# Re-timing the first group of a fused DeltaNet and maxout kernel: conversions, key-query products and substitution steps

## The chip, the cores and the metric

The kernel runs on one core of a Trainium2 chip. The metric is the device time of one execution in microseconds (us), the median of several runs. A profile is one more execution, recorded by the hardware profiler; its own time is given beside its span (from the first to the last instruction).

## The reference

Two blocks follow each other. The first is a delta-rule recurrence over 4 batches x 8 heads, 768 tokens of 48 dimensions; the second a maxout layer with three weight matrices of 384 x 768 and an output matrix of 768 x 384, applied to the 3072 tokens. Everything is float32.

```python
# attention: q, k, v are (4, 8, 768, 48), beta is (4, 8, 768)
k_n = k / (np.linalg.norm(k, axis=-1, keepdims=True) + 1e-06)
for t in range(S):
    kt, vt, bt = (k_n[:, :, t], v[:, :, t], beta[:, :, t, None])
    y[:, :, t] = np.einsum('bhd,bhde->bhe', q[:, :, t], state)
    v_old = np.einsum('bhde,bhd->bhe', state, kt)
    state = state + bt[:, :, :, None] * np.einsum('bhd,bhe->bhde', kt, vt - v_old)
# bridge: (B,H,S,D) -> (B*S, H*D), then
h = np.maximum(np.maximum(x @ w1, x @ w2), x @ w3)
return h @ w_out
```

## The kernel before

**Tiling.** The 768 tokens are cut into 12 chunks of 64, two chunks to a group; the six groups (m = 0 to 5) are pipelined. Within a chunk the recurrence becomes matrix products, so that the work on one chunk is a chain of small products. A unit is one chunk of half the batches: group m has units 4m to 4m+3. With its 4 batches a group gives 256 tokens a chunk, and the maxout layer works on 512 tokens (`TOK`) at a time: group m's maxout is interleaved with the recurrence of group m+1 and the substitution of group m+2.

**The recurrence, unit by unit and chunk by chunk.** `turn(n)` transposes the keys (part 0) or the queries (part 1) of unit n on TensorE; ScalarE copies the result. `gram(n)` (L427) multiplies keys by keys (part 0, the scores "at") and keys by queries (part 1, the masked "pt": the key-query product; the mask is a VectorE instruction, L422). The tiles at, pt, the transposed "t" and the maxout's hidden "h" share one pool of 17 buffers called "square" (L339): a new one waits until an old one's last reader is done. Then, for chunk c, come `halves_z`, `halves_u`, `join_z`, `turn_t1` and `join_u` (e, f, z, d, j: joining the inverted blocks), `old_k` and `old_q` (k, q: the state's part), `new` (u), `step` (s: the state's update), `to_y` (y) and `to_x` (x: the transposed output, input of the maxout layer). The tables `LINKS`, `EARLY_LINKS` and `FIRST` name them by such a letter and a chunk of the group (z0, z1), t and g with a unit (t0 to t3, g0 to g3).

**The substitution.** `solve(m)` (L521) inverts 32 x 32 triangular blocks of group m on VectorE: norms first, then 31 steps of two instructions (L565 multiplies into tmp, L569 subtracts from y), each bracketed by a resumption of the generator; then y goes to DRAM (L591, two DMAs) and comes back re-laid as ut (L600, eight DMAs). For m = 1 its input x and its result y lie in the SBUF space of the output weights `wo_sb`, which are written there only later: `in_wo(0)` is its first 1056 elements of a row, `in_wo(1)` the next 1056. For the other groups they are tiles of their own, `x_bl` and `y_bl`, with one buffer each. Group 0 has a shorter version, done before the stretch in question.

**The weights.** The weights come in 24 pieces of 128 x 384: for each f (128 of the 768 hidden columns) one of each of the three matrices, then six pieces of the output matrix. `fetch` (L211) issues the DMA of a piece on SyncE into one of five buffers; `weights` (L221) converts one: three ScalarE instructions (L238 to L240), and for the piece before it one VectorE shift (L250) and one integer addition on GpSimd (L254, the join). `less_first(f)` (L880) subtracts the first matrix's columns from those of the other two on VectorE (L883); the maxout uses the differences, and adds the first matrix back through `turn_first` and `both_layers`, its product with the output matrix.

**The maxout of group 0.** `ffn(m)` (L915) is a generator. A piece is one `hidden` product for one f and one difference: three products, evicted by ScalarE (L934) for the first difference and by VectorE (L938) for the second. Their PSUM tiles have two buffers, so a piece waits for the eviction of the one two before it. In group 0 four f's are done in narrow pieces of 256 tokens, first the eight for chunk 0's tokens, then the eight for chunk 1's, which need x1; f = 4 and 5 are four wide pieces of 512 tokens. Three `both_layers` products and eight half blocks of output (L959) follow. After each, control returns to the loop at L1152, whose body number i issues what the tables hold for i.

**What sets the order.** All of this stands in an order written out by hand (L95 to L1201): each engine runs its instructions in the order in which the program emits them, and each DMA queue issues in its order. The loop body emits, in this order: fetches, steps that go ahead, `FIRST`, `EARLY_LINKS`, conversions, the other steps, differences, turns of the first matrix, value scaling, and loads.

Of the kernel before, what the change touches and what calls it, by code (L numbers as in the profile page):

```python
# [23 lines left out]
def kernel(  # L24
# [177 lines left out]
                (w_t[:, :, cols], bits[:, :, f * 256 : (f + 1) * 256], (KT, 128))  # L202
            )
    bits = moe_w_out.bitcast(U32).rearrange("(t p) f -> p t f", p=128)
    for t in range(FT):
        pieces.append((wo_sb[:, t : t + 1], bits[:, t : t + 1], (1, DM)))

    staged = deque()
# [272 lines left out]
    def in_wo(i):  # L481
        n = BL * BL + BL
        return wo_sb.rearrange("p t d -> p (t d)")[:, n * i : n * (i + 1)].rearrange(
            "p (s r) -> p s r", s=2
        )
# [32 lines left out]
        )  # L518


    def solve(m):  # L521


        x = in_rows(xs[m])
        if m == 1:
            y_bl = in_wo(1)
        else:
            y_bl = work.tile([128, 2, HB * BL + HB], FP32, name="y_bl", bufs=1)
            if m > 2:
                zero = kpad[0][:, 0:1, D : D + 1]  # L530
                nc.scalar.copy(y_bl, zero.to_broadcast(y_bl.shape))
            else:
                nc.gpsimd.memset(y_bl, 0.0)
        y = in_rows(y_bl)
        bl = small("bl", BL)
        norm(bl, diagonal(x), small("root_bl", BL), small("nt_bl", BL))
        if m:
            norms_of(m, bl)
        nc.vector.reciprocal(bl, bl)
        nc.vector.tensor_tensor(out=bl, in0=bl, in1=bl, op=ALU.mult)  # L540
        nc.vector.tensor_tensor(out=bl, in0=bl, in1=beta_bl[:, m] if m else beta_0, op=ALU.mult)
        (nc.scalar.copy if m > 2 else nc.gpsimd.tensor_copy)(diagonal(y), bl)
        if m < FINE:
            size, xv, yv = HB, in_blocks(xs[m]), in_blocks(y_bl)
            xb = xv[:, :, :, 0:HB]
            by = bl.rearrange("p (s i) -> p s i", i=HB)[:, :, None, :]
            by = by.to_broadcast([128, 2, HB, HB])
        else:
            size, xv, yv = BL, x[:, None], y[:, None]
            xb, by = x, bl[:, None, :].to_broadcast([128, BL, BL])  # L550
        nc.vector.tensor_tensor(out=xb, in0=xb, in1=by, op=ALU.mult)
        yield
        for j in range(size - 1):
            a, b = j + 1, size - 1 - j
            n = BL // size
            tmp = work.tile([128, 256], FP32, name="tmp")
            t_v = tmp[:, 0 : n * a * b].rearrange("p (s c i) -> p s c i", s=n, i=b)
            row, column, rest = (
                xv[:, :, j, None, j + 1 : size],
                yv[:, :, 0:a, j, None],  # L560
                yv[:, :, 0:a, j + 1 : size],
            )
            if n == 1:
                row, column, rest, t_v = (t[:, 0] for t in (row, column, rest, t_v))
            nc.vector.tensor_tensor(  # L565
                out=t_v, in0=row.to_broadcast(t_v.shape),
                in1=column.to_broadcast(t_v.shape), op=ALU.mult,
            )
            nc.vector.tensor_tensor(out=rest, in0=rest, in1=t_v, op=ALU.subtract)  # L569
            yield  # L570
        if m == 0:
            back = in_rows(xs[0])
            nc.vector.transpose(out=back, in_=y.rearrange("p c i -> p i c"))
            yield
            for cc in range(2):
                for i in range(4):
                    bb, half = divmod(i, 2)
                    r = block(bb, half)
                    to = ut[cc][r, :, :, BL * half : BL * (half + 1)].rearrange(
                        "p g h i -> p (g h) i"  # L580
                    )
                    of = back[r, :, 16 * cc : 16 * (cc + 1)].rearrange("p i x -> p x i")
                    if half:
                        nc.scalar.copy(to, of)
                    else:
                        (nc.gpsimd if cc else nc.vector).tensor_copy(to, of)
                yield
            return
        y_d = dram.tile([2, 2, B, H, BL, BL], FP32, name="y_d")
        for cc in range(2):  # L590
            nc.sync.dma_start(  # L591
                out=y_d[cc].rearrange("f b h i j -> (f b h) i j"),
                in_=y[64 * cc : 64 * (cc + 1)],
            )
        yield
        for cc in range(2):
            for half in range(2):
                for bb in range(2):
                    r0 = C * bb + BL * half
                    (one_queue if m or cc else both_queues)[bb].dma_start(  # L600
                        out=ut[cc][
                            r0 : r0 + BL, :, :, BL * half : BL * (half + 1)
                        ].rearrange("p g h i -> p (g h) i"),
                        in_=y_d[cc, half, 2 * bb : 2 * bb + 2].rearrange(
                            "b h c i -> c (b h) i"
                        ),
                    )
            yield
# [32 lines left out]
    def halves_t(c):  # L641

        fine[c] = [square("t") for g in range(2)]
        src = [ut[c % NU][:, g].rearrange("p h x -> p (h x)") for g in range(2)]
        dst = [t.rearrange("p h x -> p (h x)") for t in fine[c]]
        nc.vector.transpose(out=dst[0], in_=src[0])
        for bb in range(2):
            nc.vector.transpose(out=dst[1][rows(1 - bb)], in_=src[1][rows(bb)])
# [266 lines left out]
    def ffn(m):  # L915
# [24 lines left out]


        early = 4 if m == 0 else 0
        for lo in (0, TOK // 2):
            for f in range(early):
                yield from hidden(f, lo, TOK // 2)
        for f in range(early, FT):
            yield from hidden(f, 0, TOK)
        if m == 0:
# [24 lines left out]
    def some(gen, n):  # L973
        for _ in range(n):
            if next(gen, gen) is gen:
                break
# [53 lines left out]
    turn(6, (0,))  # L1030
    turn(0, (1,))
    load_q(3, (nc.gpsimd, nc.gpsimd))
    nc.gpsimd.memset(in_wo(1), 0.0)
    load_beta()
    keys(6)
    gram(0, (1,), None, later=True)
# [11 lines left out]
    gram(2, (1,), None, later=True)  # L1048
    turn(3, (1,))
    some(solving, HB + 1)  # L1050
    halves_t(0)
    halves_z(0)
    gram(3, (1,), None, later=True)
# [18 lines left out]
    fetch(nc.sync)  # L1072
    halves_z(1)
    to_x(0)
    some(conv, 1)
    fetch(nc.sync)
    less_first(0)
    halves_t(1)
    for n in (2, 3):
        masked(pts[n], by_par(pts[n]))  # L1080
# [11 lines left out]
    }  # L1092
    EARLY_LINKS = {
        9: "k0 q0", 10: "t0", 11: "t1", 12: "g0", 13: "t2", 14: "g1", 15: "t3",
        16: "g2", 17: "g3", 18: "d0 d1 z0 z1", 19: "j0", 20: "j1 u0", 21: "s0",
        23: "k1 y0 q1", 24: "u1 x0", 25: "s1", 26: "y1", 28: "x1",
    }


    FIRST = {  # L1100
        0: "f1 s0 S1", 1: "z1 d1 k1 S1 S1", 2: "j1 S1 S1", 3: "q1 S1 S1",
        4: "u1 T4", 5: "y1", 6: "x1", 7: "s1 T5", 8: "T6", 9: "T7",
        14: "P4", 15: "P5", 21: "P6", 22: "P7",
    }


# [23 lines left out]
    def queries(names):  # L1130
# [8 lines left out]

    CONVERTED = {0: 2, 2: 2, 4: 2, **dict.fromkeys((1, 3, *range(5, 14), 15, 16, 19), 1)}
    FETCHED = {1: 2, 3: 2, 5: 2, **dict.fromkeys((0, 2, 4, *range(6, 12)), 1)}
    SUBSTITUTED = {
        **dict(zip(range(4, 15), (1, 1, 1, 2, 3, 3, 3, 4, 4, 3, 2))),
        **dict(zip(range(20, 31), (1, 4, 4, 3, 3, 3, 3, 4, 4, 4, 4))),
    }
    LESSENED = {1: 1, 3: 2, 5: 3, 14: 4, 15: 5}
    TURNED_FIRST = {16: (0, 1), 17: (2, 3), 19: (4, 5)}
    VALUES = {2: 2, 8: 3, 12: 4, 21: 5}  # L1150
    SCALED = {7: 2, 12: 3, 23: 4}
    for i, _ in enumerate(ffn(0)):  # L1152
        for _ in range(FETCHED.get(i, 0)):
            fetch(nc.sync)
        if i == 20:
            solving = solve(2)
        ahead = i in (13, 14, 20)
        if ahead:
            some(solving, SUBSTITUTED[i])
        queries(FIRST.get(i, ""))  # L1160
        links(1, EARLY_LINKS.get(i, ""))
        some(conv, CONVERTED.get(i, 0))
        if not ahead:
            some(solving, SUBSTITUTED.get(i, 0))
        if i in LESSENED:
            less_first(LESSENED[i])
        if i in TURNED_FIRST:
            turn_first(TURNED_FIRST[i])
        if i in SCALED:
            prep_values(SCALED[i])  # L1170
        if i in (1, 8):
            for n in range(2):
                load_k(8 + 2 * (i > 1) + n, (nc.gpsimd, nc.gpsimd))
        if i in (2, 4):
            load_q(4 + i // 2)
        if i == 11:
            load_q(11, (nc.gpsimd, nc.gpsimd))
        if i in VALUES:
            load_v(VALUES[i])
        if i == 18:  # L1180
            blocks(2)
        if i in (27, 28, 29):
            load_blocks(i - 15, nc.sync)


    RECURS.update(x=y_blocks, w=read_y, X=turn_y, p=prep_values)
# [43 lines left out]
```

## Time and profile before

| | us |
|---|---|
| median of 3 runs | 541.79 (539.97 to 544.48) |
| profiled execution, its own time | 545.26 |
| span of the profiled execution | 543.5 |
| TensorE busy | 498.7 (92%) |
| VectorE busy | 304.6 (56%) |
| GpSimd busy | 185.6 (34%) |
| ScalarE busy | 163.7 (30%) |
| group 0's first narrow piece starts | 52.6 |
| its last narrow piece starts | 119.6 |
| group 1's first piece starts | 192.6 |
| group 2's, group 3's, group 4's | 271.7, 344.4, 417.4 |

A line of a timeline gives start, duration, engine, line of the kernel, instruction, what it writes from what it reads, shapes and count; in square brackets stands how long the engine had been idle before it and what released it. PE is TensorE's matmuls, PEld its weight loads, DVE VectorE, ACT ScalarE, POOL GpSimd, SPq the DMA queue of SyncE. The granted clock is TensorE's, as a share of full speed.

### The profile page before, as it was taken

How to read it: one execution, taken by the hardware profiler on the slowest of the kernel's cores; microseconds unless marked ns; L12 is line 12 of the kernel's file. 1: busy time of each engine (PE TensorE's matmuls, PEld its weight loads, DVE VectorE, ACT ScalarE, POOL GpSimd, SP SyncE). 2: the span in 40 equal slices, each digit the busy share in tenths (PEclk: the TensorE clock that was granted, in tenths of full speed). 3: DMA queues.
4: the chain of work that ended last, by engine and by line, in shares of the span. 5: the costliest groups of instructions: out<-in, count | busy, mean ns of one | idle time of the engine just before them, and what ended most of it. 6: DMA issues, size and time to landing. Idle time of an engine off the chain costs nothing.

```text
span 543.5 us, 17974 instructions
## 1 busy us (share of the span) xinstructions
PE 498.7 (92%) x7822; PEld 310.3 (57%) x7822; DVE 304.6 (56%) x687; ACT 163.7 (30%) x303; POOL 185.6 (34%) x304
## 2 busy tenths in 40 slices
PE   6667677869899997999999999999999999999996
PEld 5556566646566653556555566555565555654453
DVE  6875956994347945179965479652989313101100
ACT  5656566744511112420024220153101331010100
POOL 7416352534371338289047774231330000000000
PEclk9855778988999997999999999999999999999999
DMA  8974295944131369255366544574333402130011
GB/s 111 207 163 122 76 181 168 184 102 87 51 75 31 93 145 161 51 154 131 101 144 122 131 130 117 123 125 89 83 80 75 80 2 60 45 72 1 0 27 31
DMA packets 110206, 53.45 MB, mean 98 GB/s; under 512 B 91760, under 2 KB 104464, under 8 KB 110128
## 3 DMA queue, kind: packets, MB, share of 16 engines
q1 hardware_dynamic: 100304, 38.37, 33.6%
q0 software_dynamic: 7712, 13.55, 11.3%
q8 instruction: 61, 1.00, 0.8%
q10 hardware_dynamic: 2112, 0.39, 0.5%
q14 instruction: 17, 0.14, 0.1%
HBM read 39.17 MB, written 13.11 MB: 96 GB/s over the span
## 4 chain that ended last, share of the span: by engine, by line
PE 77%; DVE 13%; DMA 4%; SPq 2%; issue 1%; ACT 1%; POOL 1%; ACTq 0%; DVEq 0%; POOLq 0%
PE p_h L926 33%; PE p_o L959 26%; PE p_g L438 3%; DVE tmp L565 3%; DVE wo_sb L569 2%; PE p_u L768 2%; PE p_m L906 2%; DMA kmore<-in_k_dram 2%; PE p_y L810 2%; PE p_s L791 2%; PE p_k L740 2%; DMA v_t<-in_v_dram 2%; PE p_j L723 1%; PE p_q L740 1%; SPq L120 1%; PE p_z L709 1%
## 5 line engine op out<-in xcount | busy, mean ns | idle before, releaser
L926 PE MATMUL p_h<-xt,w_sb 128*128 128x512 f32 (+1 forms) x480 | 207.4, 579 | 19.0 <-DVE w_sb L883 10.1
L926 PEld LDWEIGHTS p_h<-xt,w_sb 128*128 128x128 f32 x480 | 91.5, 199 | 100.6 <-issue 74.3
L959 PE MATMUL p_o<-wo_sb,h 128*128 128x384 f32 x288 | 98.4, 490 | 0.0
L938 DVE TENSOR_TENSOR h<-h,p_h 128x512 f32<-128x512 f32 (+1 forms) x40 | 25.3, 632 | 98.2 <-PE p_h L926 96.6
L959 PEld LDWEIGHTS p_o<-wo_sb,h 128*128 128x128 f32 x288 | 53.6, 190 | 35.3 <-issue 0.5
L565 DVE TENSOR_TENSOR tmp<-x_bl,y_bl 128x31 f32<-128x31 f32 (+20 forms) x139 | 50.3, 362 | 4.2
L934 ACT ACTIVATE h<-p_h 128x512 f32<-128x512 f32 (+1 forms) x40 | 22.1, 553 | 100.1 <-PE p_h L926 93.9
L965 ACT COPY o_sb<-p_o 128x384 f32<-128x384 f32 x24 | 11.5, 480 | 133.4 <-PE p_o L959 128.3
L959 PE MATMUL p_o<-w_sb,xt 128*128 128x384 f32 x144 | 50.4, 486 | 0.0
L569 DVE TENSOR_TENSOR y_bl<-y_bl,tmp 128x31 f32<-128x31 f32 (+20 forms) x139 | 46.3, 333 | 4.8
L396 POOL DMA_DIRECT2D turned<-in_q_dram x72 | 39.2, 552 | 6.1 <-POOL turned L391 2.6
L959 PEld LDWEIGHTS p_o<-w_sb,xt 128*128 128x128 f32 x144 | 27.4, 190 | 19.1
L438 PE MATMUL p_g<-kqt 48*64 48x64 f32 (+1 forms) x1216 | 28.7, 245 | 7.7 <-DVE nt_bl L263 3.8
L438 PEld LDWEIGHTS p_g<-kqt 48*64 48x64 f32 x1216 | 25.3, 144 | 17.5 <-ACT kqt L367 8.4
L254 POOL TENSOR_TENSOR w_sb<-mant,up 128x384 int32<-128x384 int32 x18 | 19.2, 1073 | 27.5 <-DVE mant L250 18.5
L287 POOL TENSOR_TENSOR v_t<-v_t,nrm 128x768 f32<-128x768 f32 x12 | 18.0, 1504 | 25.1 <-DVE nrm L266 11.9
L422 DVE TENSOR_TENSOR pt<-p_g,mask 128x512 f32<-128x512 f32 x20 | 13.7, 690 | 22.8 <-PE p_g L438 11.3
L120 POOL DMA_DIRECT2D kpad<-in_k_dram x32 | 21.9, 693 | 11.5 <-PE p_s L791 11.4
L798 DVE TENSOR_TENSOR st<-st,p_s 48x768 f32<-48x768 f32 (+1 forms) x18 | 17.1, 951 | 12.3 <-PE p_s L791 12.2
L391 POOL MEMSET turned<- 128x96 f32 x18 | 3.3, 191 | 54.4 <-DVE kqt L412 37.6
L455 ACT COPY at<-p_g 128x512 f32<-128x512 f32 x21 | 12.3, 585 | 31.3 <-DVE pt L422 29.5
L139 POOL DMA_DIRECT2D v_t<-in_v_dram x12 | 9.9, 830 | 31.9 <-PE p_u L768 31.4
(150 smaller groups left out, 623.9 us busy)
## 6 DMA issues: line engine op xcount, KB each, us to landing
w_bits<-in_moe_w_dram SPq DMA_DIRECT2D x18, 384.0 KB, 5.3
out_dram<-o_sb SPq DMA_DIRECT2D x48, 96.0 KB, 2.2
turned<-in_q_dram POOLq DMA_DIRECT2D x72, 48.0 KB, 2.6
kpad<-in_k_dram POOLq DMA_DIRECT2D x32, 96.0 KB, 5.3
y_x<-y SPq DMA_DIRECT2D x16, 192.0 KB
qall<-y_x SPq DMA_DIRECT2D x32, 96.0 KB, 2.6
ut<-y_d SPq DMA_DIRECT2D x40, 64.0 KB, 2.3
v_t<-in_v_dram SPq DMA_DIRECT2D x12, 192.0 KB, 4.0
```

Of the source, the lines that this page charges most:

```text
L120: queues[bb].dma_start(out=dst[rows(bb ^ g), :, 0:D], in_=src[2 * bb + g, :, c * C : (c + 1) * C, :].rearrange("h p d -> p h d"),)
L254: nc.gpsimd.tensor_tensor(out=dst.bitcast(I32), in0=mant_v.bitcast(I32), in1=up_v, op=ALU.add)
L287: nc.gpsimd.tensor_tensor(out=vts[c], in0=vts[c], in1=nrm[:, :, :, None].to_broadcast([128, 2, H, D]), op=ALU.mult,)
L396: (queue, nc.gpsimd)[i].dma_start(out=t[p0 : p0 + 32, bb, at : at + NP * 2 * D].rearrange("p (j x) -> p j x", j=NP), in_=(k, q)[i][2 * bb ...
L438: nc.tensor.matmul(p_g[rows(bb ^ (g * i)), par, c0 : c0 + C * (1 + whole)], kq[:, 0], kq if whole else kq[:, i],)
L565: nc.vector.tensor_tensor(out=t_v, in0=row.to_broadcast(t_v.shape), in1=column.to_broadcast(t_v.shape), op=ALU.mult,)
L569: nc.vector.tensor_tensor(out=rest, in0=rest, in1=t_v, op=ALU.subtract)
L798: nc.vector.tensor_tensor(out=s_v[r], in0=s_v[r], in1=p_s[r, :, 0 : H * D], op=ALU.add)
L926: nc.tensor.matmul(p_h, w_sb[i][:, t, f * 128 : (f + 1) * 128], xt[:, t, lo : lo + w], start=(t == 0), stop=(t == KT - 1),)
L934: nc.scalar.activation(out=h, in_=p_h, func=mybir.ActivationFunctionType.Relu)
L938: nc.vector.tensor_tensor(out=h, in0=h, in1=p_h, op=ALU.max)
L959: nc.tensor.matmul(p_o, stays, moves, start=(n == 0), stop=(n == len(terms) - 1))
```

## The change

Five things change together, nearly all in the part that group 0's maxout spans.

- Conversions: bodies that held two now hold one (but one body), and fetches are spread to match. The output matrix's pieces come in the order 3, 4, 5, 0, 1, 2.
- The result of substitution 1 moves from `in_wo(1)` into the `y_bl` tile, cleared on GpSimd after substitution 0 has used it; the clearing of `in_wo(1)` goes.
- Among the first four narrow pieces stand two bodies more, one after each of the first two f; the narrow pieces' loop is written in two parts for that. Body numbers after shift by two. The key-query products of units 4 and 5 (`P4`, `P5`) move from bodies 14 and 15 to 3 and 8, the query turns `T4` to `T7` from 4, 7, 8, 9 to 2, 5, 6, 7, and x1 from the body of the seventh piece to that of the sixth.
- The substitution's resumptions: those in `FIRST` (`S1`) go into `SUBSTITUTED`, which gives one or two to the early bodies and three to the later ones, always behind the body's conversion; substitution 2 gets four to a body sooner.
- `less_first` goes ahead of the steps of its body, and the first one ahead of a conversion. Several links of the table move by one body against the pieces (z0 and z1 stand behind the second wide piece instead of the third).

```diff
-    for t in range(FT):
+    for t in (3, 4, 5, 0, 1, 2):
         pieces.append((wo_sb[:, t : t + 1], bits[:, t : t + 1], (1, DM)))
...
+    ys = {}
+
+    def cleared():
+        return work.tile([128, 2, HB * BL + HB], FP32, name="y_bl", bufs=1)
+
     def solve(m):
...
-        if m == 1:
-            y_bl = in_wo(1)
-        else:
-            y_bl = work.tile([128, 2, HB * BL + HB], FP32, name="y_bl", bufs=1)
+        y_bl = ys.pop(m, None)
+        if y_bl is None:
+            y_bl = cleared()
...
-        for lo in (0, TOK // 2):
-            for f in range(early):
-                yield from hidden(f, lo, TOK // 2)
+        for f in range(early):
+            yield from hidden(f, 0, TOK // 2)
+            if f < 2:
+                yield
+        for f in range(early):
+            yield from hidden(f, TOK // 2, TOK // 2)
...
-    nc.gpsimd.memset(in_wo(1), 0.0)
...
     some(solving, HB + 1)
+    ys[1] = cleared()
+    nc.gpsimd.memset(ys[1], 0.0)
...
     to_x(0)
+    less_first(0)
     some(conv, 1)
     fetch(nc.sync)
-    less_first(0)
...
-        16: "g2", 17: "g3", 18: "d0 d1 z0 z1", 19: "j0", 20: "j1 u0", 21: "s0",
-        23: "k1 y0 q1", 24: "u1 x0", 25: "s1", 26: "y1", 28: "x1",
+        16: "g2", 17: "g3", 19: "d0 d1 z0 z1", 20: "j0", 21: "j1 u0", 22: "s0",
+        23: "k1 y0 q1", 24: "u1 x0", 25: "s1", 26: "y1", 29: "x1",
...
-        0: "f1 s0 S1", 1: "z1 d1 k1 S1 S1", 2: "j1 S1 S1", 3: "q1 S1 S1",
-        4: "u1 T4", 5: "y1", 6: "x1", 7: "s1 T5", 8: "T6", 9: "T7",
-        14: "P4", 15: "P5", 21: "P6", 22: "P7",
+        0: "f1 s0", 1: "z1 d1 k1", 2: "T4 j1", 3: "q1 P4", 4: "u1", 5: "T5 y1",
+        6: "s1 T6", 7: "x1 T7", 8: "P5", 22: "P6", 23: "P7",
...
-    CONVERTED = {0: 2, 2: 2, 4: 2, **dict.fromkeys((1, 3, *range(5, 14), 15, 16, 19), 1)}
-    FETCHED = {1: 2, 3: 2, 5: 2, **dict.fromkeys((0, 2, 4, *range(6, 12)), 1)}
-    SUBSTITUTED = {
-        **dict(zip(range(4, 15), (1, 1, 1, 2, 3, 3, 3, 4, 4, 3, 2))),
-        **dict(zip(range(20, 31), (1, 4, 4, 3, 3, 3, 3, 4, 4, 4, 4))),
-    }
-    LESSENED = {1: 1, 3: 2, 5: 3, 14: 4, 15: 5}
-    TURNED_FIRST = {16: (0, 1), 17: (2, 3), 19: (4, 5)}
-    VALUES = {2: 2, 8: 3, 12: 4, 21: 5}
-    SCALED = {7: 2, 12: 3, 23: 4}
+    CONVERTED = {6: 2, **dict.fromkeys((*range(6), *range(7, 18), 19), 1)}
+    FETCHED = {9: 2, 11: 2, **dict.fromkeys((*range(1, 9), 10, 12, 13), 1)}
+    SUBSTITUTED = dict(enumerate((1, 2, 1, 2, 1, 1, 1, 1, 2, 3, 3, 3, 3, 3, 3, 2, 2)))
+    SUBSTITUTED.update(zip(range(21, 33), (1, 4, 4, 4, 4, 4, 4, 4, 3, 3, 3, 3)))
+    LESSENED = {2: 1, 5: 2, 7: 3, 14: 4, 16: 5}
+    TURNED_FIRST = {15: (0, 1), 17: (2, 3), 20: (4, 5)}
+    VALUES = {2: 2, 8: 3, 12: 4, 22: 5}
+    SCALED = {7: 2, 13: 3, 23: 4}
...
-        if i == 20:
+        if i == 21:
             solving = solve(2)
-        ahead = i in (13, 14, 20)
+        ahead = i in (16, 21)
...
+        if i in LESSENED:
+            less_first(LESSENED[i])
         if not ahead:
             some(solving, SUBSTITUTED.get(i, 0))
-        if i in LESSENED:
-            less_first(LESSENED[i])
...
-        if i in (1, 8):
+        if i in (1, 7):
             for n in range(2):
                 load_k(8 + 2 * (i > 1) + n, (nc.gpsimd, nc.gpsimd))
-        if i in (2, 4):
-            load_q(4 + i // 2)
+        if i in (0, 1):
+            load_q(5 + i)
...
-        if i == 18:
+        if i == 19:
             blocks(2)
-        if i in (27, 28, 29):
-            load_blocks(i - 15, nc.sync)
+        if i in (28, 29, 30):
+            load_blocks(i - 16, nc.sync)
```

## The prediction

> **What bounds the kernel now.** I read first the table of the span by stretches, to see where TensorE is not full, then the timelines of TensorE and VectorE inside the stretch that isn't, then TensorE where the next group starts. In the stretches the columns are PE, PEld, DVE, ACT and POOL busy time, then the granted clock, DMA share and GB/s.
>
> ```profile
> 53.00:120.00 67.00, 49.11 (x969) 40.12 (x969) 53.68 (x118) 39.91 (x79) 28.07 (x30) 0.86 0.66 140
> 119.60:192.60 73.00, 70.76 (x1136) 45.53 (x1137) 43.43 (x108) 20.49 (x38) 26.73 (x46) 0.96 0.34 73
> 192.60:271.70 79.10, 76.31 (x1234) 44.08 (x1233) 49.65 (x110) 17.17 (x29) 43.55 (x78) 0.96 0.56 125
> 271.70:344.40 72.70, 72.70 (x1233) 42.53 (x1232) 48.26 (x115) 17.17 (x29) 43.58 (x78) 1.00 0.58 129
> ```
>
> Group 0's sixteen narrow pieces (53 to 120 us) leave TensorE 18 of 67 us idle, and VectorE is the busier engine. From 119.6 on TensorE is nearly full. Group 1 takes 79.1 us where group 2, the same work, takes 72.7: 6.4 us are lost there too. After that there is nothing to win.
>
> ```profile
> 67.33 2.93 PE L926 MATMUL p_h<-xt,w_sb 128*128 128x256 f32 x6 [3.97 <-DVE w_sb L883]
> 76.55 2.05 PE L926 MATMUL p_h<-xt,w_sb 128*128 128x256 f32 x6 [2.89 <-DVE w_sb L883]
> 86.83 2.14 PE L926 MATMUL p_h<-xt,w_sb 128*128 128x256 f32 x6 [3.19 <-DVE w_sb L883]
> 93.52 1.46 PE L926 MATMUL p_h<-xt,w_sb 128*128 128x256 f32 x6
> 110.03 1.56 PE L926 MATMUL p_h<-xt,w_sb 128*128 128x256 f32 x6 [3.46 <-DVE h L938]
> 119.60 2.93 PE L926 MATMUL p_h<-xt,w_sb 128*128 128x256 f32 x6 [3.10 <-DVE h L938]
> ```
>
> In brackets is what TensorE waited for: early on the weight differences (L883), later the evictions (L938), both VectorE's. A piece takes 1.46 us, and up to 2.93 after a wait.
>
> ```profile
> 72.95 0.36 DVE L250 TENSOR_SCALAR mant<-mant 128x384 uint32<-128x384 uint32 x1 [2.96 <-ACT mant L238]
> 82.36 0.36 DVE L250 TENSOR_SCALAR mant<-mant 128x384 uint32<-128x384 uint32 x1 [4.41 <-ACT mant L238]
> 98.50 1.09 DVE L569 TENSOR_TENSOR wo_sb<-wo_sb,tmp 128x247 f32<-128x247 f32 x1
> 99.63 0.42 DVE L565 TENSOR_TENSOR tmp<-wo_sb 128x252 f32<-128x252 f32 x1
> ```
>
> VectorE itself waits 2.96 and 4.41 us where a body holds two conversions (the second's shift needs ScalarE's multiply of the first), 3.22 for a piece at 92.1 and 0.62 at 93.2: 11.2 us of its 59.2 between 61.2 (first state update) and 120.4 (end of substitution 1), so it works 48.0. A substitution step is 2 x 0.42 us at its largest, but 1.09 instead of 0.42 while GpSimd joins a weight piece.
>
> ```profile
> 211.21 1.06 PE L709 MATMUL p_z<-ut,at 32*32 32x32 f32 x60 [2.13 <-DMA ut<-y_d]
> 212.20 5.40 PE L926 MATMUL p_h<-xt,w_sb 128*128 128x512 f32 x6
> ```
>
> This is group 1's loss: substitution 2 comes back from DRAM late, and the next piece (2.74 us elsewhere) takes 5.40.
>
> **What the Trainium skill says.** "TensorE: Matmul & The Clock Gate", Part 1 (The HAM clock gate): idleness of about a window of 3.4 us halves the matmul clock. This trace agrees in size (2.93 against 1.46 us after 3.97 us of waiting) but not as a sharp threshold (1.56 after 3.46). "SBUF — State Buffer", Who interferes with whom: a VectorE instruction with two SBUF inputs and a GpSimd one that reads SBUF exclude each other; the 1.09 against 0.42 us above agrees. "Perfetto Trace Analysis", Optimization Strategy: where the most contended engine changes over time, interleaving the regimes can help; VectorE binds to 120 us here and TensorE after.
>
> **The change part by part.** Bodies are numbered as after the change; pieces P0 to P15 are the narrow ones, P16 to P19 the wide ones.
>
> *One conversion a body, steps spread.* The 20 conversions and 34 substitution resumptions stay. The two VectorE waits of 2.96 and 4.41 go, for with one conversion each shift finds its multiply done a body earlier. But each resumption now stands behind the body's own conversion, so I count four more meetings with a join at 0.7 (1.09-0.42): +2.8 (bounds 0 and 5). Up to the end of substitution 1 VectorE also gets one conversion more (0.35 + 0.7), the difference of f=4 (about 1.3, two of 0.55 and a meeting) and the masks of P4, P5 and g1 (3 x 0.69 = 2.1), which stood behind it before: +4.4. Sum 48.0 + 4.4 + 2.8 = 55.2.
>
> *Key-query products between pieces.* Products 4 and 5 (0.69 us of TensorE each) and turns T4 to T7 (0.6 each) move into time in which TensorE waits: free there, and off the full stretch. Their masks add waits on VectorE's queue. The mask of P4 (body 3) stands behind P2, q1 and its own product; P2 waits for the difference of f=1, then 2.93 + 1.15 + 0.69 run before it: I take 3.2 us of VectorE waiting, with the later y and state additions (bodies 5, 6) and P5's mask 1.7 more: 4.9 (bounds 1 and 11). Queued behind it are a shift, a difference and steps, and TensorE waits for those differences.
>
> *Earlier differences.* The first goes ahead of a conversion and so of a join: 1.82 becomes about 1.0; VectorE starts about 0.6 sooner, at 60.6. Substitution 1 ends at 60.6 + 55.2 + 4.9 = 120.7, with waits in proportion 115 to 128, so about where it did.
>
> *What comes after it.* In before, P15 starts 0.8 us ahead of that end, with product 5 (0.69), t3 (1.1), g2 (1.1) and one turn of the first weights (0.87) still to come. After, these lie before P15: 3.7 us less remain, and P15 need not be cold (1.5). But z0 and z1 come one wide piece sooner and need the result from DRAM: before, its writes were issued at 120.49, its eight reads from 123.52 to 127.55 (the last landing, with the median of 2.7, at 130.2), 9.8 us after the end of the steps. z1 was at 139.1, so this was hidden; after, it would run from 120.7 + 9.8 = 130.5 to 131.3, against 129.9 to 130.7 in TensorE's own queue. The last pair of figures is TensorE from P13's eviction at 119.2: P15 1.5, g3 1.2, a turn 0.9, P16 and P17 5.5, z0 0.75, 0.9 waiting for the buffer that z0 frees, z1 0.75. The two are level; I take the later and 1.2 us for one piece run cold: 132.5. From z1's end to group 1 was 192.6 - 139.8 = 52.8; P18 (2.8) is now behind it: 55.6. Group 1 starts at 188.1 instead of 192.6: **-4.5** (bounds -11, where no wait of VectorE is left and TensorE binds, and +1.6, with the substitution at 128).
>
> *Substitution 2.* Its input waits, as before, for the score copy that gets its buffer from z0 (11 us from z0's end to its first norm, 137.6 to 148.65). z0 is one wide piece sooner against what follows, and product 7's mask, which held VectorE 7.10 us at 165.5 for y0, now has y0 two products behind it instead of a 3.4 us half block: about 5 saved. Steps then run 4 a body, waiting for s1 (about 4 us). Its last step, 1 us before group 1 in before, falls about 7 before it. In the SyncE queue the body that ends it now issues both the write and the eight reads ahead of the eight key loads of unit 14 (5.6 us, 193.9 to 199.5, which stood between them). Write at about -2, reads from +2 to +7 of group 1's start, landed by +9.5, needed at +14.8. The wait and the cold piece go: 2.13 + 0.63 + (5.40 - 2.74) + about 0.7 of slow products = 6.1. The key loads land at about +15 where unit 14's transposes stood at +12.8; an eviction is behind them, so I give 0.8 back: **-5.3** (bounds 0 and -6.4).
>
> *The result outside the output weights, and the new order of their pieces.* The one y_bl buffer is free when its transpose ends (29.0); the 1.0 us memset moves from 21.2 into GpSimd's idle 11.9 us before 36.3: nothing. If that cover were gone, the value scaling at 36.3 would slip by 1.0. Joins of the output weights no longer wait for the write to DRAM (6.8 idle before 124.36), at a time when TensorE was full: nothing. The joins that still overlap the input come after its last read.
>
> *Fetches and loads.* SyncE fetches come two or three bodies ahead of their conversion, as before; a body is 4 us, a fetch 5.3 to landing. Query loads 5 and 6 are issued two bodies sooner, into free buffers: nothing (bound: +2 where a key or fetch stands behind one).
>
> Sum -4.5 - 5.3 = -9.8. The profiled execution took 545.26 us (span 543.5 and 1.8 around it), so 535.5 for one like it; the median of the runs is 541.79, 3.5 below the profiled one, so **532.0** on the median.
>
> **Rivals.** *Both stretches give fully* (no VectorE waits, no cold pieces): -11 - 6 = -17, 525. For: 18 us of idle TensorE; against: masks that wait for TensorE now stand in VectorE's queue. *One of the two gives nothing* (group 0 ends even, or the result of substitution 2 is still late): -5 to -3, about 538. *The change doesn't do what it says*, the conversions still being waited for because ScalarE has queued y, turn and query copies ahead: this ends here too. *Slower:* in bodies 2 to 8 the engines take turns, VectorE waiting for a product behind a piece, the piece for a difference behind VectorE's mask. Four such hops at 5.5 us instead of the 1.2 I count put the end of substitution 1 at 138, and group 1 at 138 + 9.8 + 0.8 + 55.6 = 204.2: +11.6 - 5.3 = +6.3, 548. It decides where that end passes 126 (group 0's gain gone) and 132 (all gone). Against it: VectorE has two to three microseconds of other work in each of these bodies.
>
> **How the numbers follow.** Likeliest, 0.55: 532.0, own range 527 to 537. Fully, 0.15: 525. One only, 0.18: 538. Slower, 0.12: 548. The range reaches from the full case to past the half case and leaves out the slower one: 524 to 542. A measurement here tells about 1% (5.4 us). Over 1% faster takes the first two: 0.70; within 1% the third: 0.18; slower the last: 0.12.
>
> **What the profile after would show.** Right: no 3 to 4 us wait of a shift for ScalarE; pieces after the third at 1.46; substitution 1 ending near 121; group 1 starting near 188 and lasting about 73.5, with no wait for ut. Wrong: VectorE waiting over 5 us for products (L438), z0 or z1 waiting for ut in group 0, or a wait for the keys of unit 14 in group 1.

## The result and the profile after

The changed kernel takes 540.17 us (median of 12 runs, 538.99 to 542.22), the kernel before in the same runs 540.76: a ratio of 0.9989, 95% interval 0.9968 to 1.0009. That is no difference that can be told; 532.0 was forecast, with 527 to 537 as its range. The profiled execution after took 540.41 us (span 538.7), the one before 545.26 (543.5), 4.5 us above its own kernel's median. So the two profiles differ by more than the two kernels do.

The same four stretches in the profile after (from the last narrow piece and the first pieces of groups 1 and 2; columns as before):

```profile
53.00:120.00 67.00, 53.58 (x1046) 43.60 (x1044) 58.94 (x118) 38.91 (x78) 29.08 (x30) 0.85 0.68 148
121.70:194.00 72.30, 68.93 (x1059) 42.95 (x1060) 39.61 (x101) 19.68 (x38) 26.44 (x46) 0.93 0.31 68
194.00:266.60 72.60, 72.60 (x1234) 42.49 (x1233) 49.52 (x110) 17.05 (x29) 43.40 (x78) 1.00 0.60 135
266.60:339.30 72.70, 72.48 (x1233) 42.40 (x1232) 50.55 (x116) 17.17 (x29) 43.45 (x78) 1.00 0.57 129
```

Group 1 lasts 72.6 us, as long as group 2 (73.0), so the loss in it is gone. (It was 6.2 us rather than 6.4: group 2 starts at 271.51 in the profile before, not at 271.7, and group 1 lasts 78.9 there, not 79.1.) In the narrow stretch TensorE and VectorE both do more (53.6 and 58.9 us of 67, against 49.1 and 53.7), and TensorE runs 1046 matmuls there instead of 969, so work did move in. But group 1 starts at 194.0, not at the 188.1 of the sum, and even 1.4 later than before. The second line says where: from the last narrow piece to group 1 it takes 72.3 us, hardly less than the 73.0 of before, though 3.7 us of TensorE work had gone from it; the granted clock is 0.93 there, against 0.96. The timeline of TensorE, and then ScalarE's, around the wide pieces P16 to P19:

```profile
121.70 2.93 PE L930 MATMUL p_h<-xt,w_sb 128*128 128x256 f32 x6 [2.20 <-DVE h L942]
124.56 1.45 PE L438 MATMUL p_g<-kqt 48*64 48x64 f32 x64
126.65 5.32 PE L930 MATMUL p_h<-xt,w_sb 128*128 128x512 f32 x12
131.89 0.75 PE L713 MATMUL p_z<-ut,at 32*32 32x32 f32 x64
133.31 0.75 PE L713 MATMUL p_z<-ut,at 32*32 32x32 f32 x64 [0.67 <-ACT at L455]
135.96 5.49 PE L930 MATMUL p_h<-xt,w_sb 128*128 128x512 f32 x6 [1.90 <-ACT h L938]
```

```profile
132.67 0.59 ACT L455 COPY at<-p_g 128x512 f32<-128x512 f32 x1 [6.88 <-PE p_z L713]
133.16 0.56 ACT L238 ACTIVATE mant<-w_bits 128x384 f32<-128x384 f32 x1
133.60 0.63 ACT L239 ACTIVATE up<-w_bits 128x384 int16<-128x384 uint32 x1
134.09 0.62 ACT L240 ACTIVATE up<-w_bits 128x384 f16<-128x384 f32 x1
134.56 0.85 ACT L902 COPY w_sb<-p_t 128x384 f32<-128x384 f32 x2
135.28 0.63 ACT L938 ACTIVATE h<-p_h 128x512 f32<-128x512 f32 x1
```

The products of unit 11 (g3, at 124.56) come first, then P16 and P17 (5.32 together), then z0. Only when z0 is done does ScalarE copy the scores of unit 11 (L455, after 6.88 us of idleness: the copy waits for one of the 17 buffers, which z0 frees). Behind that copy in ScalarE's queue stand the conversion of body 17, the turned copies and only then the eviction of P16. P18 needs P16's PSUM, waits 1.90 us, and then runs cold, that is, at about half speed: 5.49 instead of 2.74. That is 4.65 us, as much as the whole gain forecast for group 0.

The same place in the profile before:

```profile
132.34 1.22 PE L438 MATMUL p_g<-kqt 48*64 48x64 f32 x64
134.19 2.74 PE L926 MATMUL p_h<-xt,w_sb 128*128 128x512 f32 x6
136.87 0.75 PE L709 MATMUL p_z<-ut,at 32*32 32x32 f32 x64
139.75 2.84 PE L926 MATMUL p_h<-xt,w_sb 128*128 128x512 f32 x6
```

```profile
138.43 0.59 ACT L455 COPY at<-p_g 128x512 f32<-128x512 f32 x1 [5.87 <-DVE pt L422]
139.84 0.60 ACT L934 ACTIVATE h<-p_h 128x512 f32<-128x512 f32 x1
```

Here one wide piece (P18, at 134.19) stands between g3 and z0 (136.87). Its eviction too sits behind the score copy, until 139.84, but the next piece, P19, needs P17's PSUM and starts without a wait. The change leaves the body number of g3 as it is while the pieces shift by two, so g3 moves up two pieces and z0 only one: now two pieces stand between them, and the third needs the first one's PSUM. (The description of the change, with links that move by one body, leaves this out.)

VectorE in the narrow stretch, after:

```profile
73.55 0.69 DVE L422 TENSOR_TENSOR pt<-p_g,mask 128x512 f32<-128x512 f32 x1 [3.35 <-PE p_g L438]
74.75 1.05 DVE L573 TENSOR_TENSOR y_bl<-y_bl,tmp 128x135 f32<-128x135 f32 x1
80.01 0.95 DVE L816 TENSOR_TENSOR y<-qs,p_y 128x768 f32<-128x768 f32 x1 [1.53 <-PE p_y L814]
88.96 1.83 DVE L887 TENSOR_TENSOR w_sb<-w_sb 128x384 f32<-128x384 f32 x2
```

and a join on GpSimd:

```profile
74.65 0.99 POOL L254 TENSOR_TENSOR w_sb<-mant,up 128x384 int32<-128x384 int32 x1 [4.60 <-DVE mant L250]
```

The waits for ScalarE are gone (one of 0.40 is left), waits for products of 3.35, 1.53 and 0.83 us have come. Substitution 1 ends at 123.1, against 120.4 before and 120.7 in the sum. Fifteen of its steps hold an instruction over 0.9 us, against eleven before. The instruction at 74.75 shows what happens (a meeting with a join): it lasts until 75.80, just past the end of the join at 75.64.

### The profile page after: what moved, and what is told of

Same layout as the page of the kernel before. It is cut to its first block, busy times and chain, and to the rows that moved or that the text cites. A ratio compares the mean times of both kernels' runs of the same rounds, so it can differ in the third digit from the quotient of the medians.

```text
span 538.7 us, 17975 instructions
## 1 busy us (share of the span) xinstructions
PE 498.6 (93%) x7822; PEld 310.7 (58%) x7822; DVE 310.8 (58%) x687; ACT 163.6 (30%) x303; POOL 185.8 (34%) x304
## 4 chain that ended last, share of the span: by engine, by line
PE 81%; DVE 12%; ACT 3%; issue 1%; DMA 1%; SPq 0%; DVEq 0%; ACTq 0%
PE p_h L930 33%; PE p_o L966 26%; PE p_g L438 4%; PE p_u L772 3%; DVE y_bl L573 2%; PE p_y L814 2%; PE p_m L910 2%; DVE tmp L569 2%; PE p_q L744 2%; PE p_s L795 2%; PE p_k L744 2%; PE p_j L727 1%; PE p_z L713 1%; PE p_t L361 1%; DVE w_sb L887 1%
## 5 line engine op out<-in xcount | busy, mean ns | idle before, releaser
L573 DVE TENSOR_TENSOR y_bl<-y_bl,tmp 128x31 f32<-128x31 f32 (+20 forms) x170 | 69.5, 409 | 5.8
L569 DVE TENSOR_TENSOR tmp<-x_bl,y_bl 128x31 f32<-128x31 f32 (+20 forms) x139 | 48.1, 346 | 4.2
L438 PE MATMUL p_g<-kqt 48*64 48x64 f32 (+1 forms) x1216 | 29.9, 251 | 7.7 <-DVE nt_bl L263 3.8
L438 PEld LDWEIGHTS p_g<-kqt 48*64 48x64 f32 x1216 | 26.5, 151 | 16.7 <-ACT kqt L367 8.3
L455 ACT COPY at<-p_g 128x512 f32<-128x512 f32 x21 | 12.3, 586 | 32.8 <-DVE pt L422 23.6
L756 DVE TENSOR_TENSOR v_t<-v_t,p_k 128x768 f32<-128x768 f32 x11 | 10.5, 951 | 16.2 <-PE p_k L744 16.1
```

The costliest lines, as they stand in the source:

```text
L438: nc.tensor.matmul(p_g[rows(bb ^ (g * i)), par, c0 : c0 + C * (1 + whole)], kq[:, 0], kq if whole else kq[:, i],)
L569: nc.vector.tensor_tensor(out=t_v, in0=row.to_broadcast(t_v.shape), in1=column.to_broadcast(t_v.shape), op=ALU.mult,)
```

## The experiments

Durations from profiles are from each kernel's own execution. "Group 0" is from its first narrow piece to group 1's first piece, "end" from that piece to the end of substitution 1. Ratios are to the kernel before in the same runs. Each duration comes from one execution, and two profiles of the same kernel differ by up to 1.7 us in "end", 1.4 in "group 0" and 5.5 in "group 1".

| kernel | ratio (95%) | end | group 0 | group 1 |
|---|---|---|---|---|
| before, first profile | | 67.8 | 140.0 | 78.9 |
| before_again | (one run, 538.54 us) | 69.5 | 139.2 | 73.4 |
| the changed kernel | 0.9989 (0.9968-1.0009) | 70.4 | 141.3 | 72.6 |
| after_again | 1.0010 (0.9986-1.0034) | 69.2 | 139.9 | 73.2 |
| g3_later | 0.9927 (0.9890-0.9964) | 69.1 | 134.7 | 72.9 |
| conv_later | 0.9987 (0.9962-1.0011) | 69.8 | 139.3 | 73.5 |
| p_back | 1.0038 (1.0011-1.0065) | 69.1 | 140.5 | 73.7 |
| two_conv | 1.0101 (1.0043-1.0158) | 70.6 | 146.4 | 72.6 |
| two_conv2 | 1.0005 (0.9970-1.0041) | 71.2 | 140.7 | 72.6 |
| tail_late | 1.0019 (0.9988-1.0049) | 68.0 | 137.8 | 72.6 |
| y_alone | 1.0002 (0.9972-1.0031) | 66.6 | 137.9 | 76.2 |
| join_last | 0.9917 (0.9883-0.9950) | 63.9 | 134.9 | 72.6 |
| g3_join | 0.9872 (0.9832-0.9913) | 63.6 | 129.6 | 72.6 |
| before_join | 0.9915 (0.9884-0.9946) | 61.9 | 131.5 | 73.9 |

**Was the first profile a usual one?** The kernel before, once more.

> The kernel before, unchanged, profiled once more. Theory A (the first profile of before caught an execution in which substitution 2 came back unusually late; the usual one loses little there): group 1 lasts 73 to 75 us instead of 79.1, the span is 539 to 540, and the 2.1 us wait for ut with the cold piece behind it is gone. Rival B (the late return is in every execution, and the changed kernel loses its gain elsewhere): group 1 lasts 78 to 80 us again and the span is 542 to 544.

Measured: span 536.8, group 1 in 73.4 us. TensorE where 2.13 us of waiting and a piece of 5.40 stood:

```profile
207.41 0.72 PE L709 MATMUL p_z<-ut,at 32*32 32x32 f32 x60 [0.22 <-DMA ut<-y_d]
208.06 2.84 PE L926 MATMUL p_h<-xt,w_sb 128*128 128x512 f32 x6
```

Theory A holds (the span is even below its 539 to 540). The late return is not a fixed cost: over the four profiles of kernels that keep the old timing of substitution 2 (with y_alone and before_join) group 1 lasts 78.9, 73.4, 76.2 and 73.9 us, in tail_late, which puts it back, 72.6; over the nine with the new timing 72.6 to 73.7, 72.9 on the mean. The five have a mean of 75.0, so the change is worth about 2 us here, on few executions, not the 5.3 read from one.

What differs with it is how long SyncE takes to issue unit 14's eight key loads, which stand ahead of the reads that bring ut: 5.59 us in the first profile and 5.50 in y_alone, where z waits 2.13 and 1.42 us; 4.43 in before_again, where it waits 0.22; 4.47 in before_join and 3.87 in tail_late, where it doesn't wait. Why the issue varies stays open.

**Does the late tail cost the changed kernel?**

```diff
-    SUBSTITUTED.update(zip(range(21, 33), (1, 4, 4, 4, 4, 4, 4, 4, 3, 3, 3, 3)))
+    SUBSTITUTED.update(zip(range(22, 33), (1, 4, 4, 3, 3, 3, 3, 4, 4, 4, 4)))
...
-        if i == 21:
+        if i == 22:
             solving = solve(2)
-        ahead = i in (16, 21)
+        ahead = i in (16, 22)
```

> The changed kernel with substitution 2 started one body later and in the numbers of steps a body that the kernel before had, so that its result goes out behind the key loads of unit 14 again. Theory A (in a usual execution the late return costs group 1 little; only the first profile of before had it badly): group 1 lasts 73 to 75 us and the median rises by 0 to 1.5 us. Rival B (the late return is costly in most executions): group 1 lasts 77 us or more and the median rises by 4 to 6 us.

Measured: 541.43 us, ratio 1.0019; the profiled execution shows no wait for ut at z and 72.6 us for group 1 (it took 535.81, the fastest of its kernel), although the key loads (189.20) go out ahead of the result (193.17) again. Rival B is out. Whether the earlier substitution is worth 0 or 2 us isn't settled: the intervals are as wide as that.

**The wait at the third wide piece.**

```diff
-        16: "g2", 17: "g3", 19: "d0 d1 z0 z1", 20: "j0", 21: "j1 u0", 22: "s0",
+        16: "g2", 18: "g3", 19: "d0 d1 z0 z1", 20: "j0", 21: "j1 u0", 22: "s0",
```

> The changed kernel with the products of unit 11 (g3) one body later, behind the first wide piece instead of ahead of it, so that the first wide piece's eviction no longer stands behind a score copy that waits for a buffer from z0. Theory A (that wait of 1.9 us and the cold piece behind it, 5.49 instead of 2.74, cost the first group 4.6 us): the third wide piece starts without a wait and takes 2.8 us, group 1 starts 3.5 to 5 us earlier and the median falls by as much, to about 536. Rival B (something else takes the wait's place at once, the mask on VectorE or the input of substitution 2): under 1.5 us.

TensorE in this kernel, in the same place:

```profile
128.77 2.84 PE L930 MATMUL p_h<-xt,w_sb 128*128 128x512 f32 x6
131.54 1.70 PE L713 MATMUL p_z<-ut,at 32*32 32x32 f32 x128
133.17 2.84 PE L930 MATMUL p_h<-xt,w_sb 128*128 128x512 f32 x6
```

No wait, no cold piece; ScalarE evicts P16 at 129.76, ahead of the score copy at 133.10. Group 0 is 5 to 6.6 us shorter than in the two profiles of the changed kernel, and the median is 536.44: ratio 0.9927, some 3.5 us better than the changed kernel's. Theory A holds, at the lower end of its size. The direct test, an eighteenth buffer in the pool, wasn't made: g3_later shows that the order of g3, P16 and z0 causes the wait, but not by itself that the pool is the reason.

**Only the conversion out of the way.**

```diff
-    CONVERTED = {6: 2, **dict.fromkeys((*range(6), *range(7, 18), 19), 1)}
+    CONVERTED = {6: 2, **dict.fromkeys((*range(6), *range(7, 17), 18, 19), 1)}
```

> The changed kernel with the conversion of body 17 moved to body 18, behind the eviction of the first wide piece instead of ahead of it on ScalarE. Theory A (between the score copy and the eviction ScalarE runs a conversion of 1.9 us that I had left out of the sum): the eviction ends 1.9 us sooner, the third wide piece's wait falls from 1.9 to about 0, and with it some or all of the cold piece: 2 to 4.6 us on the median. Rival B (the third wide piece is cold anyway, because of the waits at z1): 1.5 to 2 us at most.

```profile
132.96 1.03 PE L713 MATMUL p_z<-ut,at 32*32 32x32 f32 x64 [0.84 <-DMA ut<-y_d]
135.10 0.25 PE L713 MATMUL p_z<-ut,at 32*32 32x32 f32 x4 [1.11 <-DMA ut<-y_d]
135.55 1.06 PE L713 MATMUL p_z<-ut,at 32*32 32x32 f32 x60 [0.20 <-DMA ut<-y_d]
136.54 5.49 PE L930 MATMUL p_h<-xt,w_sb 128*128 128x512 f32 x6
```

Nothing is gained (0.9987). The eviction ends 1.88 us behind z0 instead of 3.27, but that P18 doesn't wait for it at all is owed in part to z1: in this execution, the slowest of its kernel, substitution 1 ended at 124.9 and z waited 2.15 us for its result. (With z1 done 1.4 us behind z0, as in the changed kernel, P18 would still wait some 0.5 us, an estimate.) P18 was cold all the same. This shows the next bound: the last of that result reached z at 135.55, 10.7 us behind the end of the substitution, with nothing left between.

**The key-query products back in their old places.**

```diff
-        0: "f1 s0", 1: "z1 d1 k1", 2: "T4 j1", 3: "q1 P4", 4: "u1", 5: "T5 y1",
-        6: "s1 T6", 7: "x1 T7", 8: "P5", 22: "P6", 23: "P7",
+        0: "f1 s0", 1: "z1 d1 k1", 2: "T4 j1", 3: "q1", 4: "u1", 5: "T5 y1",
+        6: "s1 T6", 7: "x1 T7", 16: "P4", 17: "P5", 22: "P6", 23: "P7",
```

> The changed kernel with the key-query products of units 4 and 5 back where they stood against the pieces before the change (bodies 16 and 17). Theory A (their masks, standing in VectorE's queue behind a cold piece, hold up the weight differences and the steps: 3.35 us in body 3): substitution 1 ends 3 to 5 us sooner, the third and fifth narrow pieces start 1 to 3 us sooner, but two products of 0.69 us return into the full stretch: 1 to 3 us faster. Rival B (the moved products are worth more than their waits cost): no wait of VectorE for products in body 3, but the same or up to 2 us slower.

```profile
75.33 0.42 DVE L942 TENSOR_TENSOR h<-h,p_h 128x256 f32<-128x256 f32 x1 [3.10 <-PE p_h L930]
```

Theory A falls: without the mask VectorE waits 3.10 us for the piece that comes next, where it had waited 3.35 for the product. The end is hardly sooner and the kernel 0.4% slower than the one before. Against the changed kernel's two ratios the moved products are worth 1.5 to 2.6 us, at the edge of what the intervals tell, and their waits cost nothing that shows.

**Two conversions a body again.**

```diff
-    CONVERTED = {6: 2, **dict.fromkeys((*range(6), *range(7, 18), 19), 1)}
+    CONVERTED = {0: 2, 3: 2, 6: 2, **dict.fromkeys((1, 4, *range(7, 16), 17, 18, 21), 1)}
```

> The changed kernel with two conversions again in the bodies of the first, third and fifth narrow piece and none in the two new bodies. Theory A (one conversion a body removes VectorE's waits for ScalarE, 2.96 and 4.41 us before the change): waits of the shift for ScalarE of 2 to 4 us come back, substitution 1 ends 2 to 5 us later and the median rises by 2 to 4 us. Rival B (those waits lie where VectorE has to wait for a piece anyway): within 1.5 us.

It is 1.0% slower, but not by theory A: the end stays (70.6). My edit had put the last conversion into body 21, and the first product of both layers waited for its join:

```profile
150.97 5.49 PE L910 MATMUL p_m<-wo_sb,w_sb 128*128 128x384 f32 x8 [3.20 <-POOL wo_sb L254]
```

So the test was made again with bodies 7 to 19 left as the change has them (the wording of its expectation on the sixth piece means only this):

```diff
-    CONVERTED = {6: 2, **dict.fromkeys((*range(6), *range(7, 18), 19), 1)}
+    CONVERTED = {0: 2, 3: 2, 6: 2, **dict.fromkeys((1, 4, *range(7, 18), 19), 1)}
```

> The changed kernel with two conversions in the bodies of the first, third and fifth narrow piece and none in the two new bodies and the sixth piece's place of the plan kept, as in the run before, but from body 7 on exactly as the changed kernel, so that no conversion of an output weight comes late for the products of both layers. Theory A (one conversion a body saves VectorE 2 to 5 us): substitution 1 ends at 125 or later and the median rises by 2 to 4 us. Theory B, after the run before (substitution 1 ended at 123.2 with two and at 123.1 with one): the end stays within 1 us of 123 and the median within 1.5 us of the changed kernel's.

1.0005, end 71.2: theory B. VectorE's waits are 4.48, 3.81 and 0.83 us for a product, a state product and ScalarE, 9.1 together against 6.1 in the changed kernel; two of the differences take 1.02 instead of 1.83. One conversion a body, the part first named, is worth nothing here that the medians show.

**The result outside the output weights, alone on the kernel before** (its diff is that part of the change: the order of the pieces, `ys`, `cleared` and the moved memset).

> The kernel before with one part of the change alone: the result of substitution 1 in its own tile, cleared on GpSimd after substitution 0, and the output weights' pieces in the order 3, 4, 5, 0, 1, 2. Theory A (it lies where the engines concerned are idle): median within 1.5 us of the kernel before. Rival B (GpSimd's 6.8 us wait ahead of 124.36 held ScalarE's conversions and the turns behind them): 1.5 to 3 us faster.

1.0002: nothing, as the prediction had it.

**The order inside a body.** If the steps meet joins because they follow the shift, the conversion should come last.

```diff
-        some(conv, CONVERTED.get(i, 0))
         if i in LESSENED:
             less_first(LESSENED[i])
         if not ahead:
             some(solving, SUBSTITUTED.get(i, 0))
+        some(conv, CONVERTED.get(i, 0))
```

> The changed kernel with the order inside a body turned round: differences first, then substitution steps, the conversion last. No step then follows directly on the shift that releases a join on GpSimd. Theory A (in group 0's narrow pieces VectorE is held by meetings with joins, 0.7 us in nearly every body, and twice in a difference): the 1.0 to 1.1 us steps among 0.4 us ones and the 1.83 us differences become rare, substitution 1 ends 6 to 10 us sooner than its 123.1, the third, fifth and seventh narrow pieces start 1 to 2 us sooner. As the wait for a buffer at the third wide piece stays, the median falls by 2 to 5 us. Rival B (VectorE then waits for TensorE instead; the narrow pieces are held by the chain of small products): substitution 1 ends at most 3 us sooner and the median stays within 1.5 us.

Theory A holds: the end comes 5.3 to 6.5 us sooner than in the two profiles of the changed kernel, seven steps instead of fifteen hold an instruction over 0.9 us, and the median is 534.93. From its first state update to that end VectorE works 49.1 us instead of 56.2 and waits 6.7 instead of 6.1: it is the work that shrank. The third wide piece still waits 1.90 us and takes 4.54. VectorE in g3_join, the version with both edits: the step that met a join at 74.75 in the changed kernel (the first two lines), and a meeting that is left, with its join:

```profile
74.13 0.29 DVE L569 TENSOR_TENSOR tmp<-wo_sb,y_bl 128x135 f32<-128x135 f32 x1
74.46 0.30 DVE L573 TENSOR_TENSOR y_bl<-y_bl,tmp 128x135 f32<-128x135 f32 x1
75.38 0.35 DVE L250 TENSOR_SCALAR mant<-mant 128x384 uint32<-128x384 uint32 x1
75.65 0.41 DVE L942 TENSOR_TENSOR h<-h,p_h 128x256 f32<-128x256 f32 x1
75.98 1.09 DVE L569 TENSOR_TENSOR tmp<-wo_sb,y_bl 128x175 f32<-128x175 f32 x1
```

```profile
75.88 1.00 POOL L254 TENSOR_TENSOR w_sb<-mant,up 128x384 int32<-128x384 int32 x1 [2.41 <-DVE mant L250]
```

The step runs at 0.30 instead of 1.05. The shift at 75.38 releases the join; the eviction behind it takes its usual 0.41, and only the next step meets the join (1.09).

**Both edits.**

> Both: the products of unit 11 one body later and the conversion last in each body. Theory A: the gains add, as they are in different stretches: 5 to 8 us below the changed kernel, about 533 where the kernel before is 539.6. Rival B: with the substitution sooner, the first cause is partly gone (z0 no longer waits), or the wide pieces become the only bound: no more than the later products give alone, 3 us.

533.40 us, ratio 0.9872: the gains add as theory A had it, and this version beats the kernel before by 1.3% and the changed one by about as much. Group 0 lasts 129.6 us.

**The order inside a body, on the kernel before.**

```diff
-        some(conv, CONVERTED.get(i, 0))
+        if i in LESSENED:
+            less_first(LESSENED[i])
         if not ahead:
             some(solving, SUBSTITUTED.get(i, 0))
-        if i in LESSENED:
-            less_first(LESSENED[i])
+        some(conv, CONVERTED.get(i, 0))
```

> The kernel before with only the order inside a body turned round: differences first, then steps, the conversion last. Theory A (the meetings with joins are the largest removable cost of the narrow pieces in this kernel too, where 8 steps from body 6 on take 1.03 us or more): substitution 1 ends 3 to 6 us sooner and the median falls by 2 to 4 us. Rival B (in the kernel before VectorE waits for ScalarE and TensorE in the same places, so that a shorter VectorE only waits longer): under 1 us.

0.9915, and the end comes 5.9 to 7.6 us sooner than in the two profiles of the kernel before: the size of theory A. Its reason is shown only in part. All five differences of the loop take 1.0 us, and nine steps instead of eleven hold an instruction over 0.9 us, but VectorE's work falls by only 1.6 to 2.0 us; its waits, for ScalarE and for pieces, fall from 11.2 and 12.5 to 6.9. The edit also puts the differences ahead of the steps, and which of the two moves shortens the waits wasn't separated. These few lines, without any of the change, give more than the change does.

**The changed kernel once more.**

> The changed kernel, unchanged, once more. Theory A (group 0 loses at the third wide piece what it gains before it, in every execution): the third wide piece waits 1.5 to 2.5 us for ScalarE's eviction and takes 4 to 5.5 us, group 1 lasts 72.5 to 73.5, the median is within 0.4% of the kernel before. Rival B (the wait was chance): the third wide piece starts without a wait, group 1 starts at 189 or sooner.

1.0010; P18 again waits 1.90 us and takes 5.49. Theory A: the loss is in both executions profiled. The same wait (1.89 to 1.91 us) stands in the profiles of p_back, two_conv, tail_late and join_last, which leave g3 where the change put it, with P18 taking 4.12 to 4.54.

## Why the prediction was wrong

**What bounds the kernel.** Right on the narrow stretch; wrong on group 1. I took its length from one execution whose own time stood 3.5 us above the median of the runs, and carried that difference along as an offset instead of asking where it lay. It lay where I put more than half of the gain.

**Substitution 2 (-5.3).** The steps came much as worked out: the last one 5.4 us ahead of group 1 (7 forecast), the write and the reads ahead of unit 14's key loads, z found the result there, group 1 takes 72.6 us (73.5 forecast). The term was mis-sized: it is the difference to one unusual execution. Against the five profiles with the old timing it is worth 2 us on the mean, and tail_late shows none of it.

**VectorE up to the end of substitution 1.** The working of the order was close: work 56.2 us (55.2), waits 6.1 (4.9, of which the first mask 3.35 against 3.2), end 123.1 (120.7). More meetings with joins came, as counted. One term was added up wrongly: a difference of two times 0.55 with a meeting of 0.7 is 1.8, not 1.3 (1.84 measured at f = 4), and the difference of f = 3, without a meeting before, met one (1.83). But I booked the removed waits for ScalarE as a gain and the new waits for products as a cost; in p_back a wait for a product only gives way to one of like length for a piece, and in two_conv2 2.3 us less work meets 3.0 us more waiting. What holds this stretch in the changed kernel is the meetings: putting the conversion last took 5.3 to 6.5 us off the end.

**What comes after it (-4.5).** This step failed. I gave z1's wait for z0's buffer 0.9 us (0.67 measured) and 1.2 for a cold piece, then let P18 follow at once. I had seen that the score copy waits for z0, but not followed ScalarE's queue behind it: the conversion, the turned copies and the eviction, 2.65 us from the copy's end to 135.91, with P18 waiting for the last. With g3 two pieces up and z0 one, P16's eviction had come to stand in that queue, and P18 two pieces behind P16. It cost 1.90 + 2.75 us. P15 came 2.5 us late and cold besides (2.93). So z1 ended at 134.1 instead of 132.5, and from there to group 1 it took 59.9 us instead of 55.6: together the 5.9 us by which group 1 started late. g3_later takes the wait and the cold piece away. That its group 1 then starts at 188.3, so near to the sum's 188.1, is partly luck, for P15 is late and cold there too.

**Nothing for the rest.** y_bl and the order of the weight pieces: right (y_alone). The moved products: right in sign, 1.5 to 2.6 us (p_back).

**The signs.** Of the three signs of being wrong only a trace appeared in this profile, 0.46 us of VectorE's waiting for unit 14's keys (the longest wait for products was 3.35 us, and z had its result in time): the loss lay on ScalarE's queue, which none of them watched. One of the signs of being right failed: of the pieces after the third, those at 73.41 and 92.28 took 2.93 and 2.58 us, not 1.46.

**Rivals.** The nearest was "one of the two gives nothing", at 538. Its two causes are about what happened, both in part at once: group 0 ended even, and group 1's gain was small in a usual execution. The slower rival, the engines taking turns, was not seen: its decision point was an end past 126, and it came at 123.

## What to carry to other kernels

Where an instruction is delayed, follow everything behind it on its own engine until the next one that TensorE needs; waiting for a buffer is such a delay, and reordering moves who stands behind it. Where an instruction on one engine lengthens those of another, as the joins did here (1.05 us instead of 0.30), put work that it doesn't lengthen right behind the instruction that releases it, and the rest ahead. And don't book a stall as a gain from one profiled execution that is slower than the median.

## What the runs showed of the hardware

A cold piece doesn't follow from the length of the wait ahead of it alone. In the first profile of before P13 ran in 1.56 us after 3.46 us of waiting, in before_again in 2.93 after 3.47; P18 took 5.49 after 1.90, with 0.67 of waiting and two groups of small products just before it.

What a join lengthens differs by instruction. In g3_join two joins ran from 84.41 to 86.38, and the eviction at 84.45, which reads one input from PSUM, took 0.42 us as elsewhere; steps and differences, with both inputs in SBUF, were stretched (1.05 instead of 0.30, 1.83 instead of 1.02). So was a shift in the changed kernel, though it has only one input: 0.97 us instead of 0.35 at 86.09, with a join from 85.84 to 86.85.

The executions of the kernel before spread from 535.5 to 545.7 us. Over the 128 of them that ran beside the experiments the longer ones had the lower granted clock (correlation -0.67); which is the cause of which isn't shown.
